# One sine half, one bank and two numerator groups moved at the start of a cosine-weighted attention and SwiGLU kernel

## The chip, the cores and the metric

The kernel runs on one core of one Trainium2 chip. A core has five engines that run at the same time, each with its own queue of instructions that it takes in order: TensorE (PE in the profile, with its weight loads as PEld), VectorE (DVE), ScalarE (ACT), GpSimd (POOL) and SyncE (SP). Instructions on different engines wait for each other through semaphores. Matrix products land in PSUM, which this kernel uses as seven banks: `psA` (two), `psG`, `psV` and `psC` (two each). DMAs are issued by SP or by POOL and run on 16 DMA engines. The metric is the time of one execution in microseconds on the device; lower is better.

## The reference

Two layers follow each other. The first is linear attention with cosine weights, for 8 batches, 8 heads, 576 positions, head size 64:

```python
phi(x) = concat(max(x, 0) * cos_w, max(x, 0) * sin_w)      # 64 -> 128 features
kv  = sum over s of phi(k)[s, f] * v[s, d];   z = sum over s of phi(k)[s, f]
out = (phi(q) @ kv) / (phi(q) @ z + 1e-6)
```

The second takes the 4608 rows of 512 (8 batches of 576), normalises each by its root mean square and a weight `g`, and applies a SwiGLU feed-forward with 1536 inner columns: `(silu(xn @ w_gate) * (xn @ w_val)) @ w_out`. Inputs and output are float32; the kernel multiplies in bfloat16.

## The kernel before, in words

**Blocks.** The feed-forward works on blocks of 512 rows. Block b (0 to 7) holds 512 rows of batch b as four tiles of 128; block 8 holds the batches' remaining 64 rows and runs between blocks 6 and 7. A block has 12 steps n = 0 to 11, each computing 128 of the 1536 inner columns, four matmuls for the gate into `psG[n % 2]` and four for the value into `psV[n % 2]` (L556); ACT takes the Silu of the gate (L575) and DVE multiplies it with the value into `hT` (L576). Then come four output steps, 12 to 15, of 12 matmuls each (L579) into `psC`, whose result ACT copies out (L286) and SP stores (L590, or L597 in block 0). The input of a block is `xnT`, the normalised rows transposed; there are two such buffers, used in turn, and every matmul of L556 reads all four tiles of its block.

**Attention alongside.** While block b is multiplied, the attention of batch b + 1 is made ready in between. A helper `at(blk, n, where, f, ...)` puts a piece of work into a slot of a step: "pe" ahead of the step's matmuls, "pre" behind them, "post" behind the step's own ACT and DVE work, or, in output steps, behind the store. Entries of one slot run in the order in which `at` was called. Each engine executes what it is given in this written order. The pieces for batch nb:

- `k_phi` (L292 on ACT for the sine half, L294 on DVE for the cosine half), `v_cast`, and `kvz_pe`, which makes kv and z in `psA`.
- `q_phi`: the two halves of phi of one q tile, then the transposition into `qpT`: by a DMA transpose (`q_tr_dma`, L346), or, for batch 1, by PE into a bank (`q_tr_pe`, L363) and a copy out of it (`q_tr_evac`).
- `nd_pe` (L449): numerators and denominators of one q tile, 8 matmuls into `psA`. `nd_post`: DVE's reciprocal and product (L489, L492, L499) into `xt`, which frees `psA` again.
- `x_sq` (ACT, L515) and a power on POOL (L520) for the root mean square; `x_norm` (DVE, L527); `x_tr_dma` (L540), a DMA transpose issued by SP into the next block's `xnT`.
- `load_kv` and `load_q`: the loads of a later batch, 1 MB or a little more each, issued by SP (by POOL for the first batches) into a ring of five buffers.

**Around the change.** Batch 1 is prepared late in block 0. Its last value step, `last_step`, makes kv, the numerators of q tile 0 and, in `q_tr(2, psV[0])`, the transposition of q tile 2. Block 0's output, `out_first`, is 48 matmuls numbered i = 0 to 47 over four banks; ahead of certain i stand pieces of batch 1: at 6, 11 and 19 the numerators of tiles 1, 2 and 3, at 9 the transposition of q tile 3, at 43 the last tile's transposition by PE into `psV[0]`.

Batch 2 is prepared in block 1. Its numerators stand ahead of steps 6, 8, 9 and 11, and the normalisation and `x_tr_dma` of each follow one step later (two for the first). In the "post" slot of step 12 stands also SP's load of batch 3's q (`load_q`, 1 MB), and in that of step 13 the load of a pair of q tails. For the later batches the steps are 4, 6, 8 and 10.

Of the kernel before, what the change touches and what calls it, by code (L numbers as in the profile page):

```python
# [17 lines left out]
def kernel(  # L18
# [28 lines left out]
    V, A, G = nc.vector, nc.scalar, nc.gpsimd  # L47
# [11 lines left out]
    psV = [ps.tile([P, 512], FP32, name=f"psV{i}") for i in range(2)]  # L59
# [15 lines left out]
    def wide(b):  # L75
        return b > 2
# [681 lines left out]
    def at(blk, n, where, f, *args):  # L758
        slots.setdefault((blk, n), {}).setdefault(where, []).append((f, args))
# [9 lines left out]
        at(0, 5 + c // 3, "post", k_phi, A, 1, c, 1)  # L769
    for j in range(4):  # L770
        at(0, (8, 8, 9, 10)[j], "post", q_phi, V, 1, j, 0)
        at(0, 8 + j, "post", q_phi, A, 1, j, 1)
        bank = (psC[0], psC[1], psV[0], psV[1])[j]
        if j < 2:
            at(0, 10 + j, "pe", q_tr_pe, 1, j, bank)
            at(0, 10 + j, "pre", q_tr_evac, V, 1, j, bank)
# [42 lines left out]
    for j, i in ((1, 6), (2, 11), (3, 19)):  # L819
        at(0, 12, i, x_first, j)  # L820
        at(0, 12, i, x_last, j - 1)
    at(0, 12, 9, q_tr, 3, psV[1])
    at(0, 12, 21, x_norm, 1, 3)
    at(0, 12, 21, load_q, 2)
    at(0, 12, 43, x_tr, 3, psV[0])
    for nb in range(2, B):
        b = nb - 1
        first = nb == 2
        for i, cs in enumerate(KCS5 if wide(nb) else KCS):
            kb, kn = ((0, 14), (0, 15), (1, 0), (1, 1))[i] if first else (b - 1, 12 + i)  # L830
            for c in cs:
                at(kb, kn, "post", k_phi, V, nb, c, 0)
                at(kb, kn, "post", k_phi, A, nb, c, 1)
        for i in range(2):
            vb, vn = ((0, 15), (1, 0))[i] if first else (b - 1, 13 + 2 * i)
            at(vb, vn, "post", v_cast, V, nb, (2 * i, 2 * i + 2))
        for j in range(4):
            late = j + (nb == 3)
            qb, qn = (b, 1 + j) if first else (b - (late < 2), (14 + late) % 16)
            at(qb, qn, "post", q_phi, V, nb, j, 0)  # L840
            at(qb, qn, "post", q_phi, A, nb, j, 1)
            at(qb, qn, "post", q_tr_dma, nb, j)
        kz = 3 if first else 2
        at(b, kz, "pe", kvz_pe, nb)
        at(b, kz, "pre", kvz_evac, A, nb)
        for j in range(4):
            n = ((6, 8, 9, 11) if first else (4, 6, 8, 10))[j]
            at(b, n, "pe", nd_pe, nb, j)
            at(b, n, "pre", nd_post, nb, j)
            at(b, n, "post", x_sq, nb, j)  # L850
            m = n + 2 if first and j == 0 else n + 1
            at(b, m, "post", x_norm, nb, j)
            at(b, m, "post", x_tr_dma, nb, j)
# [107 lines left out]
```

## Time and profile before

| what | value |
|---|---|
| median of 3 runs | 323.7 us (323.67 to 324.08) |
| the profiled execution | 323.82 us, span 322.0 us |
| mean granted TensorE clock | 0.999 |
| PE busy | 316.3 us, 98% of the span |
| DVE busy | 186.2 us, 58% |
| ACT busy | 166.0 us, 52% |
| POOL busy | 40.8 us, 13% |
| SP's DMA queue (q1) | 73110 packets, 41.25 MB, 62.6% of 16 engines' span |
| POOL's DMA queue (q0) | 6944 packets, 12.13 MB, 15.5% |

How to read the profile's lines. A row of the table of engines gives busy time, its share of the span, and the number of instructions. The chain that ended last is followed back from the last instruction to whatever released it, and is printed in order of time as start, length, engine, tile and line; while one engine is the bound, nearly all of it is on that engine. A timeline row has start, length, engine, line, operation, tiles (written tile first), the number of instructions merged, and in brackets the idle time of the engine before it and what ended it. "SPq" marks SP's issuing of a DMA: its length is that of the issue, and the transfer lands later. A row of DMA issues gives the transfer, its size and the time from issue to landing. A row of a window gives, for a stretch of time, its length, the busy time of PE, PEld, DVE, ACT and POOL with the number of instructions in brackets, the granted TensorE clock as a share of full speed, the share of the DMA engines and GB/s. All times count from the start of the span.

In time order: the stretch up to 33 us makes batch 0's attention and begins block 0; block 0's output runs from 42 to 55 us, block 1's value steps from 55 to 78 us, its output from 78 to 88 us, and block 2 begins at 88.3 us.

### The profile page before, as it was taken

What the parts mean: (1) busy time and instruction counts of PE and PEld (TensorE: products, weight loads), DVE (VectorE), ACT (ScalarE), POOL (GpSimd) and SP (SyncE); (2) the same over time, 40 slices, a digit from 0 to 9 for tenths busy, and PEclk for the clock granted to TensorE, in tenths of its full rate; (3) what the DMA queues carried; (4) which work ended last, traced back from release to release, by engine and by line L of the source; (5) the groups of instructions that cost most, each with busy time, mean ns of one, the idle gap of its engine ahead of it and who ended that gap; (6) DMA issues with size and microseconds to landing.
All of it is one profiled execution on the core that took longest, in us unless ns stands there. A gap on an engine that the chain in (4) does not pass through costs nothing.

```text
span 322.0 us, 6059 instructions
## 1 busy us (share of the span) xinstructions
PE 316.3 (98%) x2310; PEld 162.2 (50%) x2310; DVE 186.2 (58%) x382; ACT 166.0 (52%) x322; POOL 40.8 (13%) x79
## 2 busy tenths in 40 slices
PE   7899999999999999999999999999999999999996
PEld 2689564544455445444544445544544444444444
DVE  7976977768447772777457655781676034204420
ACT  5766665754575457455745575446544333223321
POOL 9771211002001100011001100100011000000000
PEclk9999999999999999999999999999999999999999
DMA  7999999778999989999799959994522500041002
GB/s 228 239 269 269 282 328 209 219 168 179 214 224 224 204 244 203 231 246 167 159 195 215 211 153 198 206 217 154 107 53 47 116 33 0 0 100 33 1 35 98
DMA packets 80091, 53.76 MB, mean 167 GB/s; under 512 B 52234, under 2 KB 74046, under 8 KB 80062
## 3 DMA queue, kind: packets, MB, share of 16 engines
q1 hardware_dynamic: 73110, 41.25, 62.6%
q0 software_dynamic: 6944, 12.13, 15.5%
q8 instruction: 18, 0.29, 0.4%
q14 instruction: 11, 0.09, 0.1%
q10 hardware_dynamic: 8, 0.00, 0.0%
HBM read 37.83 MB, written 9.44 MB: 147 GB/s over the span
## 4 chain that ended last, share of the span: by engine, by line
PE 94%; DMA 2%; ACT 1%; POOL 1%; DVE 1%; issue 0%; POOLq 0%; ACTq 0%
PE psC L579 27%; PE psG L556 27%; PE psV L556 27%; DMA vv<-in_v_dram 2%; PE psV L648 2%; PE psA L449 2%; PE psG L648 2%; PE psA L387 2%; PE psG L579 1%; PE psA L394 1%; PE psV L363 1%; PE psA L474 0%; ACT scr L515 0%; PE psG L430 0%; PE psC L546 0%; POOL raw L135 0%
## 5 line engine op out<-in xcount | busy, mean ns | idle before, releaser
L576 DVE TENSOR_TENSOR hT<-psV,sg 128x512 bf16<-128x512 f32 x99 | 68.2, 689 | 96.4 <-PE psV L556 64.9
L556 PE MATMUL psV<-xnT,wv 128*128 128x512 bf16 x352 | 90.3, 379 | 0.0
L556 PE MATMUL psG<-xnT,wg 128*128 128x512 bf16 x352 | 90.3, 379 | 0.0
L575 ACT ACTIVATE sg<-psG 128x512 f32<-128x512 f32 x99 | 58.6, 592 | 60.5 <-PE psG L556 57.7
L579 PE MATMUL psC<-wo,hT 128*128 128x512 bf16 (+1 forms) x408 | 88.8, 376 | 0.0
L579 PEld LDWEIGHTS <-hT 128*128 128x128 bf16 x456 | 43.1, 98 | 47.7
L556 PEld LDWEIGHTS <-wv 128*128 128x128 bf16 x400 | 39.0, 98 | 47.0
L556 PEld LDWEIGHTS <-wg 128*128 128x128 bf16 x400 | 36.9, 98 | 39.6 <-issue 0.2
L520 POOL TENSOR_TENSOR rs<-ms,mhalf 128x1 f32<-128x1 f32 x36 | 20.6, 572 | 194.1 <-ACT scr L515 193.9
L286 ACT COPY osb<-psC 128x512 f32<-128x512 f32 x32 | 18.8, 586 | 49.9 <-PE psC L579 49.9
L515 ACT ACTIVATE scr<-xt 128x513 bf16<-128x513 f32 x36 | 22.8, 634 | 22.6 <-DVE xt L499 21.7
L527 DVE SCALAR_TENSOR_TENSOR xn<-xt,rs,gb 128x512 bf16<-128x512 f32 (+1 forms) x37 | 26.9, 731 | 9.9 <-POOL rs L520 9.8
L292 ACT ACTIVATE kp<-raw,tab 128x256 bf16<-128x256 f32 (+2 forms) x51 | 28.8, 607 | 2.4 <-DMA raw<-in_k_dram 2.4
L499 DVE TENSOR_TENSOR xt<-psA,rec 128x512 f32<-128x512 f32 x36 | 24.9, 692 | 1.2
L292 ACT ACTIVATE qp<-raw,tab 128x512 bf16<-128x512 f32 (+1 forms) x36 | 23.4, 666 | 1.9 <-DMA raw<-in_q_dram 1.9
L294 DVE TENSOR_SCALAR kp<-raw,tab 128x256 bf16<-128x256 f32 (+2 forms) x53 | 20.2, 428 | 0.6 <-DMA raw<-in_k_dram 0.6
L294 DVE TENSOR_SCALAR qp<-raw,tab 128x512 bf16<-128x512 f32 (+1 forms) x34 | 15.5, 468 | 4.4 <-DMA raw<-in_q_dram 4.4
L449 PEld LDWEIGHTS <-qpT 128*128 128x128 bf16 x224 | 10.5, 97 | 7.0 <-DMA qpT<-qp 0.5
L288 DVE CAST vv<-raw 116x1280 bf16<-116x1280 f32 (+1 forms) x13 | 11.5, 881 | 1.8 <-DMA raw<-in_v_dram 1.8
L556 PE MATMUL psV<-xnT_tail,wv 128*128 128x512 bf16 x48 | 12.3, 379 | 0.0
L556 PE MATMUL psG<-xnT_tail,wg 128*128 128x512 bf16 x48 | 12.3, 379 | 0.0
L449 PE MATMUL psA<-kvzs,qpT 128*128 128x65 bf16 x224 | 11.4, 193 | 0.0
(102 smaller groups left out, 178.4 us busy)
## 6 DMA issues: line engine op xcount, KB each, us to landing
out_dram<-osb SPq DMA_DIRECT2D x27, 256.0 KB, 2.3
raw<-in_q_dram SPq DMA_DIRECT2D x6, 1024.0 KB, 9.2
raw<-in_k_dram SPq DMA_DIRECT2D x5, 1120.0 KB, 8.7
raw<-in_v_dram SPq DMA_DIRECT2D x5, 1120.0 KB, 9.7
raw<-in_k_dram POOLq DMA_DIRECT2D x2, 1152.0 KB, 19.4
raw<-in_v_dram POOLq DMA_DIRECT2D x2, 1152.0 KB, 15.9
out_dram<-osb SPq DMA_DIRECT2D x17, 128.0 KB, 2.6
wg<-in_moe_w_gate_dram POOLq DMA_DIRECT2D x3, 512.0 KB, 13.9
```

What stands on the lines that cost most here:

```text
L286: A.copy(out=o, in_=i)
L292: A.activation(out=out_ap, in_=in_ap, func=AF.Relu, scale=scale)
L294: eng.tensor_scalar(out=out_ap, in0=in_ap, scalar1=scale, scalar2=0.0, op0=ALU.mult, op1=ALU.max)
L449: nc.tensor.matmul(heads[:, g, hp, :], lhsT=qpT[:, h, j * P : (j + 1) * P], rhs=kvzs[b][:, g, hp * E : (hp + 1) * E], start=True, stop=True,)
L499: V.tensor_tensor(out=xt[:, 0:DM].rearrange("p (hp g d) -> p g hp d", g=2, d=D), in0=heads[:, :, :, 0:D], in1=rec[:, :, :].unsqueeze(3).to ...
L515: A.activation(out=scr[:, :], in_=xt[:, 0 : DM + 1], func=AF.Square, scale=1.0 / math.sqrt(DM), accum_out=ms[:, :],)
L520: G.tensor_tensor(out=rs[:, :], in0=ms[:, :], in1=mhalf[:, :], op=ALU.pow)
L527: V.scalar_tensor_tensor(out=xn_of[(b, j)][:, c], in0=x_of[(b, j)][:, c], scalar=rs_of[(b, j)][:, :], in1=gb[:, c], op0=ALU.mult, op1=ALU. ...
L556: nc.tensor.matmul(bank[:, cols[0] : cols[1]], lhsT=w[:, t, n * P : (n + 1) * P], rhs=x[:, t, cols[0] : cols[1]], start=(t == 0), stop=(t ...
L575: A.activation(out=sg[:, :], in_=g[:, 0:TB], func=AF.Silu)
L576: V.tensor_tensor(out=hT[:, n, :], in0=v[:, 0:TB], in1=sg[:, :], op=ALU.mult)
L579: nc.tensor.matmul(bank[:, 0 : cols[1] - cols[0]], lhsT=hT[:, n, j * P : (j + 1) * P], rhs=wo[:, n, cols[0] : cols[1]], start=(n == 0), st ...
```

## The change

Three constants and one bank differ.

- The sine half of phi of batch 1's q tile 3, on ACT, moves from the end of step 11 of block 0 (`last_step`) to the end of step 10, directly behind the same half of tile 2.
- The transposition of that tile by PE goes into `psV[0]`, which tile 2's used just before, and no longer into `psV[1]`.
- In block 1, the numerators of batch 2's tiles 2 and 3 go from steps 9 and 11 to steps 10 and 12. With them move `nd_post`, `x_sq`, and, one step behind, `x_norm` and `x_tr_dma`: for tile 2 to step 11, for tile 3 to step 13.

```diff
     for j in range(4):
         at(0, (8, 8, 9, 10)[j], "post", q_phi, V, 1, j, 0)
-        at(0, 8 + j, "post", q_phi, A, 1, j, 1)
+        at(0, (8, 9, 10, 10)[j], "post", q_phi, A, 1, j, 1)
...
-    at(0, 12, 9, q_tr, 3, psV[1])
+    at(0, 12, 9, q_tr, 3, psV[0])
...
         for j in range(4):
-            n = ((6, 8, 9, 11) if first else (4, 6, 8, 10))[j]
+            n = ((6, 8, 10, 12) if first else (4, 6, 8, 10))[j]
             at(b, n, "pe", nd_pe, nb, j)
             at(b, n, "pre", nd_post, nb, j)
             at(b, n, "post", x_sq, nb, j)
             m = n + 2 if first and j == 0 else n + 1
             at(b, m, "post", x_norm, nb, j)
             at(b, m, "post", x_tr_dma, nb, j)
```

## The prediction

> **What bounds the kernel now.** I read the page's table of engines first, then the chain that ended last around the two places that the diff touches (42 to 46 us; 71 to 97 us), then SP's instructions in order of time, because SP issues the transposes there, and last the landings of single transfers.
>
> From the page, then the chain in order of time (start, length, what):
>
> ```profile
> PE 316.3 (98%) x2310; PEld 162.2 (50%) x2310; DVE 186.2 (58%) x382; ACT 166.0 (52%) x322; POOL 40.8 (13%) x79
> ...
> 43.78 0.73 ACT scr L515 x2
> 44.50 0.62 ACT qp L292
> 45.12 0.04 issue
> 45.17 0.62 PE psV L363 x8
> ...
> 70.35 0.24 PE psA L449 x8
> ...
> 71.45 0.86 PE psV L556 x4
> 72.32 0.32 PE psA L449 x8
> ...
> 78.06 10.36 PE psC L579 x48
> 88.42 0.86 PE psG L556 x4
> ...
> 96.55 0.42 PE psA L449 x8
> ```
>
> PE is the bound, 98% busy: an edit pays only where the chain leaves PE, and hurts only where it makes PE wait. The chain leaves PE at 43 to 45 us: the transposition of q tile 3 (L363) follows ACT's sine half (L292). At 72.32 a numerator group takes 0.32 us where an undisturbed one takes 0.24 (70.35); at 96.55 0.42. Block 2 follows block 1's output matmuls at 88.42 with no gap.
>
> SP's instructions in order of time:
>
> ```profile
> 75.12 1.02 SPq L115 DMA_DIRECT2D raw<-in_v_dram  x2
> 76.23 2.63 SPq L540 DMA_TRANSPOSE xnT<-xn  x2
> 81.30 0.38 SPq L590 DMA_DIRECT2D out_dram<-osb  x1
> 81.77 1.22 SPq L540 DMA_TRANSPOSE xnT<-xn  x1
> 83.08 0.53 SPq L126 DMA_DIRECT2D raw<-in_q_dram  x1
> 83.89 0.36 SPq L590 DMA_DIRECT2D out_dram<-osb  x1
> 84.30 1.87 SPq L145 DMA_DIRECT2D rqt<-in_q_dram  x2
> ...
> 107.29 0.57 SPq L126 DMA_DIRECT2D raw<-in_q_dram  x1
> 109.40 5.31 SPq L540 DMA_TRANSPOSE xnT<-xn  x2
> ```
>
> Now the transpose of batch 2's fourth tile (81.77; I call it T) goes out **ahead** of batch 3's 1 MB q load (83.08). At 107 us another transpose goes out **behind** such a load, and how long each took, from issue to landing, is in the answers for their own stretches (q load at 107.29, transpose at 109.40, transpose at 73.80 with little queued ahead):
>
> ```profile
> raw<-in_q_dram SPq DMA_DIRECT2D x1, 1024.0 KB, 10.3
> ...
> xnT<-xn SPq DMA_TRANSPOSE x1, 8.6
> ...
> xnT<-xn SPq DMA_TRANSPOSE x1, 2.6
> ```
>
> 107.29+10.3 = 117.6 and 109.40+8.6 = 118.0: the transpose behind the load landed 0.4 us after it, not 2.6 us after its own issue. The stores agree: the one of 81.30 took 5.9 us (lands 87.2), that of 83.89, behind the q load, 7.4 (91.3), the tail load of 84.30 7.6 (91.9). The q load itself landed by 90.6, where DVE's wait for it ends (4.44 us before 90.61). So SP's transfers land very nearly in the order of issue.
>
> **The change part by part.** The sum is made against the profiled execution: 323.82 us with a span of 322.0, 0.1 above the median 323.7.
>
> *Sine half earlier, other bank.* One ACTIVATE of 0.71 us (L292) moves from 44.40 to behind the third's (38.26, ending 38.97). ACT idles 0.97 us there, until the Silu of 39.94 gets its bank, so 38.97 to 39.68 hides; if that idle time were missing, the Silu and PE's last output matmuls would be later by up to 0.71. At its old place ACT then just waits longer for xt (45.65). The transposition needs DVE's cosine half (ended 40.83) and the first value bank, whose previous content ACT copied out by 43.88 (42.87+1.01); PE reaches it at 44.86 (44.21 plus three matmuls of 0.216). So it starts at 44.86, not 45.17: 0.31 us at most. The next group is late no more than that: it needs xt of 44.85+0.69 = 45.54 and would come at 45.75. But block 1, at 54.59, loads weights 0.17 us late, and the third transpose of its input, issued at 50.28 with 4.2 us to landing, lands at 54.5. Its predecessors were delayed by POOL's batch-2 v load, issued at 39.18 and not moved. Gain between 0.05 and 0.31; I take 0.1, as the landing is the nearest limit.
>
> *Numerators spaced.* Tile 2's group goes one step on, tile 3's from the last value step to the first output step, with their xt, square, pow (POOL is idle over 1 us before each) and normalisation. PE's 0.08 us at 72.32 goes, since the xt that it waited for (71.49+0.69) is then long done. Tile 2's transpose moves from 77.6 to about 79.7 us and still queues behind the v load of 75.12 (8.6 us to landing, 83.7): costs nothing; without that load it would arrive 2 us later, with 8 to spare.
>
> *Tile 3 and SP's queue.* Before, step 12 of block 1 (its first output tile) issues store 0, T and the q load; T leaves for step 13, behind store 1. New order: store 0, q load, store 1, T, tail load. T's input: ACT's copy ends at 81.28, square and accumulator 0.82, pow 0.55, normalisation 0.75 give 83.4 to 83.7; store 1 holds SP until 84.25; T issues at 84.3 to 85.5. ACT's copy for store 1 had 0.78 us of idle time, so the inserted square costs it 0.04. Until T lands PE can't begin block 2 (every matmul there reads all four tiles), and behind PE's first weight load stands all the rest.
>
> Where does T land? The transfers up to and including T are the same set that ended with store 1 before, at 91.3. Lower bound: T can't land before the q load and store 1 have gone, and even the q load landed at 90.6 with T ahead of it; freed of T (the second of 85 to 86 us moved only 115 GB/s, the four after it 297 to 349) it gains some 1.2, then store 1 costs 256 KB at 340 GB/s = 0.8, and T its 1.2: 91.4 again, less what overlaps. Ends: 90.3 (all of T's length overlapped) and 91.9 (the next entry's landing). I take 91.0, less the 0.1 gained above, since the v load is issued relative to PE. PE starts 0.05 us after a landing (the transpose issued at 91.35 landed 5.2 us later, at 96.5, and released the group of 96.55): 90.95 against 88.26 for block 2's first matmul: **+2.7**. The 0.08 doesn't count then, as the landing sets the start. The q load lands about 1.1 us earlier, so batch 3's q tiles come earlier and PE's wait at 96.55 goes: 0.42-0.24 = **-0.2**. From there the chain shows PE alone.
>
> *Clock.* PE would idle from 87.9 to 90.95, some 3 us; the longest gap now in mid-kernel is about 1.1. At the end of the kernel the windows (PE busy in column 2, granted clock after POOL) show:
>
> ```profile
> 319.20:321.50 2.30, 0.04 (x1) 0.00 (x0) 0.26 (x1) 0.00 (x0) 0.00 (x0) 1.00 0.37 114
> 321.50:322.00 0.50, 0.00 (x0) 0.00 (x0) 0.00 (x0) 0.00 (x0) 0.00 (x0) 0.71 0.00 0
> ```
>
> 0.71 over half a us is full speed for 0.2 and half speed for 0.3: the clock halved 2.45 us after PE's last matmul. At the start, ten warm-up matmuls of 634 ns median (379 later) took 3.84 us, the last of them already at 379: full speed came after about 3.2 us of work. So a 3 us gap may halve the clock, and 3.2 us of work at half speed cost 1.6. Ends 0 and 1.7; I take **+1.6**, as 3 is beyond 2.45, though not by much, and one row says nothing of the phase.
> [...]
>
> Sum: 323.82 + 2.7 - 0.2 + 1.6 = 327.9, against the median of runs 327.8.
>
> **The rivals.**
> 1. *The same wait without the halved clock.* [...] 323.7+2.7-0.2 = 326.2, from 325.5 to 327.1 with T's bounds. [...]
> 2. *Not slower: T isn't held by the q load.* The place is the start of block 2. T issued at 84.3 with 2.6 us (transpose of 73.80) lands at 86.9; with 4.2 (50.28) at 88.5. Up to 88.2 PE loses nothing, and the time is 323.7-0.1-0.1-0.2 = 323.3, at best 323.1. Against it: 117.6 and 118.0, and 91.3 for a store issued right behind the same q load.
>    [...]
> 3. *A short wait.* T lands between 88.6 and 90, by overlap with the store and the load: 324 to 325.4, gap too short for the clock.
> 4. *A longer wait.* T takes the 8.6 us of the one at 109.40: 92.9, +4.6; 323.7+4.6-0.2+1.6 = 329.7.
>
> **How the numbers follow.** Chances: forecast 0.46, rival 1 0.34, rival 2 0.10, rival 3 0.05, rival 4 0.05. Predicted 327.8. Range 325.5 (rival 1, T at 90.3) to 328.9 (forecast, T at 91.9, clock 1.7); it leaves out rivals 2, 3 and 4. 0.2% is 0.65 us, about what can be told from no change. Rival 2 gives 323.1 to 323.6, mostly within that: faster 0.03, same 0.08, slower 0.89.
>
> **What would show it.** After: L292's fourth sine half near 39 us with nothing of ACT ahead of the transposition at 44.9; block 1's start within 0.3 us of before. SP: the q load at about 81.7, T at about 84.3, and T's landing near 91. PE idle some 3 us between the last output matmul of block 1 and L556 near 91, released by the transpose into xnT; a granted clock under 1.00 and 634 ns matmuls in the 3.4 us behind it. The group near 96 no longer released by qpT. Wrong if T lands before 88.2, if the idle stretch leaves the clock at 1.00 (then 326.2), or if later blocks show waits that they don't have now.

## The result and the profile after

The changed kernel takes 325.04 us (median of 8 runs, 324.64 to 325.46), the kernel before 323.89 us (8 runs, 323.0 to 324.58): a ratio of 1.0037, 95% interval 1.0024 to 1.005, so some 1.2 us slower. The profiled execution took 324.64 us with a span of 322.9. A second profile of each stands beside these below, from the experiments.

The table of engines and the chain in order of time, at the two places of the change:

```profile
PE 314.4 (97%) x2274; PEld 162.3 (50%) x2310; DVE 185.3 (57%) x382; ACT 166.0 (51%) x322; POOL 40.5 (13%) x79
...
43.97 0.65 PE psG L579 x3
44.62 0.45 PE psV L363 x8
45.06 0.43 PE psG L579 x2
...
69.62 0.24 PE psA L449 x8
...
82.81 0.72 DVE vv L288
83.53 5.54 DMA xnT<-xn
89.07 0.14 issue
89.21 1.02 PE psG L556 x4
...
97.51 0.25 PE psA L449 x8
```

The trace has 36 matmul records fewer than that of before (x2274 against x2310) for the same matmuls, so the two busy times of PE can't be compared. The sine half no longer stands in the chain: the transposition at 44.62 follows the three output matmuls ahead of it without a gap. But the chain now leaves PE from 73 to 89 us, and its longest stretch off PE there is a transfer: T, the transpose of batch 2's fourth tile, issued at 83.53 and landed at 89.07. (That the value cast of the `L288` row released T is the profile's inference; T's issue follows directly behind SP's issue of store 1, and in a run below T goes out at 83.90 before the same cast ends at 83.99.) Block 2's first matmul, at 88.26 before, is at 89.21, although everything ahead of it runs 0.7 us earlier than in the profile of before (0.4 of that from the first 35 us, where executions differ, 0.3 from the sine half).

SP's instructions, and what PE waited for (in total, times, longest):

```profile
80.49 0.38 SPq L590 DMA_DIRECT2D out_dram<-osb  x1
80.96 0.39 SPq L126 DMA_DIRECT2D raw<-in_q_dram  x1
83.08 0.36 SPq L590 DMA_DIRECT2D out_dram<-osb  x1
83.53 1.23 SPq L540 DMA_TRANSPOSE xnT<-xn  x1
```

```profile
PE psG L556 <- DMA xnT<-xn: 1.6, 1, 1.6
```

The order is the one that the diff makes: store 0, batch 3's q load, store 1, T. PE waits 1.6 us for T, once. The windows around that gap (PE's busy time in the second column, the granted clock after POOL's):

```profile
83.00:87.40 4.40, 4.40 (x22) 1.88 (x20) 2.18 (x5) 1.88 (x4) 0.00 (x0) 1.00 1.08 352
87.40:89.20 1.80, 0.22 (x1) 0.02 (x1) 0.47 (x1) 1.55 (x3) 0.00 (x0) 1.00 1.37 206
89.20:92.00 2.80, 2.74 (x12) 1.27 (x14) 0.80 (x2) 1.48 (x4) 0.00 (x0) 1.00 1.14 273
```

The clock stays at 1.00 through the gap and behind it.

### The profile page after: what moved, and what is told of

Read it like the earlier page. It is cut to its first block, busy times and chain, and to the rows that moved or that the text cites. A ratio compares the mean times of both kernels' runs of the same rounds, so it can differ in the third digit from the quotient of the medians.

```text
span 322.9 us, 6022 instructions
## 1 busy us (share of the span) xinstructions
PE 314.4 (97%) x2274; PEld 162.3 (50%) x2310; DVE 185.3 (57%) x382; ACT 166.0 (51%) x322; POOL 40.5 (13%) x79
## 4 chain that ended last, share of the span: by engine, by line
PE 89%; DMA 4%; DVE 3%; issue 2%; POOL 1%; ACT 1%; ACTq 0%; POOLq 0%; DVEq 0%
PE psV L556 26%; PE psG L556 26%; PE psC L579 24%; PE psV L648 2%; DMA vv<-in_v_dram 2%; PE psG L579 2%; PE psA L449 2%; PE psG L648 2%; PE psA L387 2%; DMA xnT<-xn 2%; DVE xn L527 1%; PE psA L394 1%; ACT scr L515 1%; PE psA L474 0%; PE psV L363 0%
## 5 line engine op out<-in xcount | busy, mean ns | idle before, releaser
L556 PE MATMUL psG<-xnT,wg 128*128 128x512 bf16 x337 | 88.5, 379 | 2.3 <-DMA xnT<-xn 1.6
L556 PE MATMUL psV<-xnT,wv 128*128 128x512 bf16 x344 | 89.6, 379 | 0.7 <-issue 0.2
L556 PEld LDWEIGHTS <-wv 128*128 128x128 bf16 x400 | 39.0, 98 | 47.0
L556 PEld LDWEIGHTS <-wg 128*128 128x128 bf16 x400 | 37.0, 98 | 41.7 <-issue 2.3
L556 PE MATMUL psV<-xnT_tail,wv 128*128 128x512 bf16 x48 | 12.3, 379 | 0.1
L556 PE MATMUL psG<-xnT_tail,wg 128*128 128x512 bf16 x46 | 12.0, 379 | 0.1
L288 DVE CAST vv<-raw 116x1280 bf16<-116x1280 f32 (+1 forms) x13 | 11.1, 857 | 0.0
```

Of the source, the lines that this page charges most:

```text
L556: nc.tensor.matmul(bank[:, cols[0] : cols[1]], lhsT=w[:, t, n * P : (n + 1) * P], rhs=x[:, t, cols[0] : cols[1]], start=(t == 0), stop=(t ...
```

## The experiments

Each run is compared with the kernel before on the same chip: 323.53 us (median of 23 runs) for the sine half with the bank, the spaced numerators alone, the steps 6, 8, 10, 11 and the q load behind T; 323.45 (13) for the q load ahead of T in the kernel before, the q load by POOL and the two further loads; 323.69 (23) for the sine half alone, the second profiles and the steps 5, 7, 9, 11.

### The parts alone

The sine half and the bank without the spaced numerators:

```diff
-            n = ((6, 8, 10, 12) if first else (4, 6, 8, 10))[j]
+            n = ((6, 8, 9, 11) if first else (4, 6, 8, 10))[j]
```

> The change without the spaced numerators: only ACT's sine half and the bank. Theory (the wait comes from the spacing alone): no wait of PE before block 2, the transposition starts at the end of the three matmuls ahead of it, 0.31 us earlier than before, and all of it is kept, as the profile of the changed kernel has block 1 begin 0.3 us earlier against its own start: 323.6 us against 323.9. Rival, the prediction's reading (block 1's start is held by the third transpose into its input): 0.1 us, 323.8. Rival (the sine half or the bank bears part of the loss): 324.2 or more.

Measured: 323.32 us, ratio 0.9989, interval 0.9977 to 1.0. The wait ahead of block 2 is not there, and block 2 begins near 87.5. The chain shows the same two rows as the changed kernel:

```profile
43.92 0.65 PE psG L579 x3
44.56 0.45 PE psV L363 x8
```

The sine half alone, with the transposition left in the second bank (`psV[1]`):

> The sine half moved, the transposition still in the second value bank, numerators as before. Theory (the bank bears no part): PE reaches the transposition with both halves and the bank ready, as with the first bank: 323.3 us, 0.3 under the kernel before. Rival (the first bank is what frees the transposition): the second bank is read by DVE until 44.2 us, so it waits, and the time stays at the kernel before's 323.5.

Measured: 323.26 us, ratio 0.9989, interval 0.9978 to 0.9999. The chain has the same rows once more:

```profile
43.58 0.65 PE psG L579 x3
44.22 0.45 PE psV L363 x8
```

So the bank bears no part. In the chains, the time from block 0's first `L556` row to block 1's is 21.94 us in the profile of before (32.97 to 54.91), 21.62 in the changed kernel (32.57 to 54.19) and 21.63 here (32.17 to 53.80): the sine half gives 0.3 us.

The spaced numerators alone (sine half and bank as before):

> Only the spaced numerators; sine half and bank as before. Theory: T lands behind batch 3's q load and store 1, PE waits for it ahead of block 2 for 1.3 to 1.7 us, and the parts add up: 0.3 us above the changed kernel, 325.3. Rival (the landing is a fixed time that the 0.3 us earlier PE only waits out): the same as the changed kernel, 325.0, with a wait of 1.3 us.

Measured: 325.02 us, ratio 1.0043, interval 1.0029 to 1.0057. T is issued at 84.00 and lands at 89.5, PE waits 1.5 us. So the loss is the spacing's. Against its own before this is 1.4 to 1.5 us, 0.2 to 0.3 more than the changed kernel's 1.2, as adding up would have it, but the intervals don't tell the two expectations apart.

### Tile 3's place or tile 2's?

Numerators ahead of steps 6, 8, 10 and 11, so that only tile 2 moves:

```diff
-            n = ((6, 8, 10, 12) if first else (4, 6, 8, 10))[j]
+            n = ((6, 8, 10, 11) if first else (4, 6, 8, 10))[j]
```

> Numerators of batch 2 ahead of steps 6, 8, 10 and 11, so tile 2 is spaced and tile 3 stands where it stood, T ahead of the q load. Theory (only T's place in SP's queue costs): no wait ahead of block 2; 0.3 us from the sine half and 0.08 from the numerators' wait at step 9: 323.5 us. Rival (tile 2's later transpose is what comes late): a wait ahead of block 2 as in the changed kernel, near 325.

Measured: 324.03 us, ratio 1.0015, interval 1.0005 to 1.0026. Neither expectation: there is no wait ahead of block 2, but a new one in front of tile 3's numerators. The timeline of DVE and PE there:

```profile
74.24 0.74 DVE L527 SCALAR_TENSOR_TENSOR xn<-xt,rs,gb 128x512 bf16<-128x512 f32 x1
74.90 0.16 DVE L489 TENSOR_SCALAR rec<-psA 128x8 f32<-128x8 f32 x1
75.09 0.20 DVE L492 RECIPROCAL rec<-rec 128x8 f32<-128x8 f32 x1
75.33 0.69 DVE L499 TENSOR_TENSOR xt<-psA,rec 128x512 f32<-128x512 f32 x1
...
76.07 0.40 PE L449 MATMUL psA<-kvzs,qpT 128*128 128x65 bf16 x8 [0.58 <-DVE xt L499]
```

Tile 1's normalisation now stands on DVE ahead of tile 2's division, which frees `psA` only at 76.02, one step after tile 2's numerators. Two groups one step apart cost 0.08 us of waiting in the kernel before, and 0.58 here.

### Is it the place behind the q load?

T where the change put it, but the q load issued directly behind T:

```diff
             at(b, m, "post", x_tr_dma, nb, j)
+            if first and j == 3:
+                at(b, m, "post", load_q, 3)
...
-                at(b, n, "post", load_q, nb)
+                if nb > 3:
+                    at(b, n, "post", load_q, nb)
```

> The changed kernel, but SP issues batch 3's q load directly behind T and not ahead of it; T's own issue stays where the change put it, near 83.5 us. Theory (SP's queue is served in order, T waits for the 1 MB ahead of it): T lands near 87, PE doesn't wait ahead of block 2, the q load lands 2.5 us later than in the changed kernel and PE's wait for batch 3's first q transpose near 96 us is back at 0.2 to 0.5: 323.7 us. Rival (T is late because it is issued one output step later, whatever stands ahead): it lands near 89 as in the changed kernel and the time stays 325.0.

Measured: 325.14 us, ratio 1.0043, interval 1.0029 to 1.0057. On T the theory holds: issued at 83.90, no earlier than in the changed kernel, it is in time, and block 2 begins at 87.81 with no wait. Store 1 is issued ahead of T here as in the changed kernel, so the store alone isn't what makes T late. On the time it fails. The q load, issued at 85.21, takes 7.0 us and lands at 92.2. What PE waits for now, and ACT's timeline behind it:

```profile
PE psG L556 <- ACT sg L575: 0.8, 1, 0.8
...
PE psA L449 <- DMA qpT<-qp: 0.5, 1, 0.5
```

```profile
92.19 0.72 ACT L292 ACTIVATE qp<-raw,tab 128x512 bf16<-128x512 f32 x1 [2.98 <-DMA raw<-in_q_dram]
92.82 0.58 ACT L575 ACTIVATE sg<-psG 128x512 f32<-128x512 f32 x1
```

ACT stands 2.98 us at batch 3's first sine half, and block 2's Silu, queued behind it, keeps its gate bank from PE for 0.8 us; the q transposes come 0.5 us late as well. So both transfers have a deadline near the start of block 2, and neither order on SP's queue served both with T issued at 83.5 to 83.9.

The reverse in the kernel before: nothing moved but the q load, one step earlier, ahead of T.

```diff
-        for which, n in zip("kvq", {1: (4, 8, 12), 2: (3, 5, 8)}.get(b, (0, 3, 6))):
+        for which, n in zip("kvq", {1: (4, 8, 11), 2: (3, 5, 8)}.get(b, (0, 3, 6))):
```

> The kernel before, with batch 3's q load one step earlier (step 11 of block 1), so ahead of T, which keeps its place and its issue at 81 to 82 us; nothing else is changed. Theory: T, though issued as early as before, lands behind the 1 MB, near 88.3 to 89.5 us against a start of block 2 near 88; PE waits 0.3 to 1 us: 323.9 to 324.5 us against 323.5. Rival (the later issue of T is what costs): no wait, 323.5.

Measured: 323.99 us, ratio 1.0016, interval 1.0005 to 1.0027. T, issued at 82.43, is over 1 us earlier than in the changed kernel and late all the same: PE has a gap of 0.69 us ahead of block 2, in the chain

```profile
87.91 0.69 issue
88.59 1.02 PE psG L556 x4
```

T's issue did come 1.0 us later against block 2 than in the kernel before, since SP took 1.55 us over the issue of store 0 ahead of it. But here T went out 5.5 us before block 1's output was done (87.91) and came late; with the place ahead of the q load it was in time when it went out 3.9 us before block 2's start (83.90 and 87.81). So the place decides.

### A queue of its own for the q load

The changed kernel with batch 3's q load issued by POOL:

```diff
-                at(b, n, "post", load_q, nb)
+                at(b, n, "post", load_q, nb, *((G,) if nb == 3 else ()))
```

> The changed kernel with batch 3's q load issued by POOL, at the same place in the order of work, so that it no longer stands in SP's queue; T is issued by SP near 83.5 us as in the changed kernel, with store 1 alone ahead of it. Theory (order within SP's queue): T shares the DMA engines with the q load but doesn't follow it, lands between 86 and 88 us, PE waits 0 to 0.5 us ahead of block 2: 323.4 to 324.3 us, if the q load itself isn't later than 90 us. Rival (the DMA engines' bytes decide, not the queue): T lands near 89 and the time stays 325.0.

Measured: 327.13 us, ratio 1.0133, interval 1.0079 to 1.0187. The theory in its narrow form falls, and the rival too, as the time isn't 325.0 but more. T is issued at 83.73 and PE starts at 91.28. The q load by POOL (issued at 81.87):

```profile
raw<-in_q_dram POOLq DMA_DIRECT2D x1, 1024.0 KB, 8.6
```

It lands at 90.4, T some 0.8 us behind, going by PE's start. Another queue didn't let T pass: the load that was issued first landed first, here too, and it took longer (8.6 us from issue to landing, against 6.4 in the changed kernel, from 80.96 to the end of DVE's wait for it at 87.39). Why T stayed behind a load on another queue is not shown: this run changed the queue alone. The windows of this run:

```profile
87.80:90.30 2.50, 0.00 (x0) 0.00 (x0) 0.00 (x0) 1.21 (x2) 0.00 (x0) 1.00 1.40 209
90.30:91.20 0.90, 0.00 (x0) 0.00 (x0) 0.49 (x1) 0.72 (x1) 0.00 (x0) 0.52 1.31 211
91.20:97.10 5.90, 5.60 (x13) 2.05 (x15) 1.08 (x2) 1.71 (x4) 0.00 (x0) 0.50 1.00 148
97.10:99.00 1.90, 1.90 (x44) 1.52 (x43) 1.08 (x2) 0.70 (x2) 0.00 (x0) 0.99 0.72 138
```

PE's gap is 3.5 us, and the clock halves 2.5 us into it and stays so for 6.8 us. Of these, 0.9 us fall in the gap; the other 5.9 us are work at half speed and cost 2.9 us, an estimate from the clock of 0.50. This execution took 330.07 us with a mean granted clock of 0.99, the three others 326.6, 326.7 and 327.5 with 1.0, 1.0 and 0.995.

### How long a gap halves the clock?

The changed kernel with a further load directly behind the q load, into a buffer that nothing reads: 0.5 MB, and 0.75 MB.

```diff
+    extra = one.tile([P, 4, 4 * D], FP32, name="extra")
+    def load_extra():
+        nc.sync.dma_start(out=extra[:, :, :], in_=q_rows(3)[:, 0:4, :])
...
                 at(b, n, "post", load_q, nb)
+                if nb == 3:
+                    at(b, n, "post", load_extra)
```

> The changed kernel with a further load of 0.5 MB (half of batch 3's q rows, into a buffer that nothing reads) directly behind the q load and so ahead of T. Theory: T lands 1.5 us later at 330 GB/s, PE's wait ahead of block 2 grows from 1.6 to 3.1 us and the time by as much, 326.5, with the clock at full speed. Rival, the prediction's reading of the kernel's end (the clock halves 2.45 us after PE's last matmul): the granted clock is 0.5 in the 3 us behind the wait, 634 ns matmuls, 1.6 us more, 328.1.

> As the 0.5 MB load, with 0.75 MB. Theory: T lands 2.3 us later than in the changed kernel, PE waits 3.9 us, 327.3 with the clock at full speed throughout. Rival (2.45 us of idle PE halve the clock): 328.9 and a granted clock of 0.5 behind the wait. If this one shows the halved clock and the 0.5 MB one doesn't, the limit lies between 3.1 and 3.9 us, or depends on where the wait falls in some period.

Measured: 329.35 us for 0.5 MB (ratio 1.0166, interval 1.0116 to 1.0217; single runs 326.64, 329.1, 329.61, 329.95) and 329.11 us for 0.75 MB (1.0186, 1.0146 to 1.0225; 328.77 to 330.69). The profiled executions (326.64 and 329.34 us), 0.5 MB first:

```profile
87.60:90.80 3.20, 0.02 (x1) 0.00 (x0) 0.49 (x1) 1.81 (x3) 0.00 (x0) 1.00 1.22 286
90.80:94.20 3.40, 3.25 (x15) 1.57 (x17) 1.08 (x2) 1.73 (x4) 0.00 (x0) 1.00 1.15 252
```

```profile
87.80:91.80 4.00, 0.19 (x1) 0.00 (x0) 0.49 (x1) 1.82 (x3) 0.00 (x0) 1.00 1.19 298
91.80:95.20 3.40, 3.04 (x7) 1.17 (x9) 0.00 (x0) 1.21 (x2) 0.00 (x0) 0.50 1.17 258
95.20:97.00 1.80, 1.80 (x10) 0.79 (x9) 1.08 (x2) 0.67 (x2) 0.00 (x0) 0.99 0.00 0
```

A gap of 3.3 us left the clock at full speed in the profiled execution. A gap of 3.9 us halved it, at its very end, for 3.4 us of work. The three other runs with 0.5 MB are 2.5 to 3.3 us longer than the profiled one. Their mean granted clocks are known, though their gaps aren't: 0.995, 0.99 and 0.99, against 0.999 for the profiled run. A mean of 0.994 goes with the 3.4 us at half speed of the profiled 0.75 MB run, 0.99 with the 6.8 us of the POOL run. So, going by the means, the clock halved in three of the four runs with 0.5 MB, and in all four with 0.75 MB (0.99 to 0.994): one and the same kernel does both. Both loads moved T as the queue's order has it: PE's gap grew from 1.6 us by 1.7 and 2.3.

### Second profiles, and a variant

> The kernel before, for a second profile. The prediction took T's place from one execution, in which store 0 landed at 87.2 us, the q load at 90.6 and store 1 at 91.3, 0.8, 2.3 and 3.0 us from the start of block 2 at 88.3. Theory (that execution had a slow stretch of the DMA queue): here the q load lands within 1.6 us of block 2's start, as in the run with the sine half alone (89.1 against 87.5). Rival (it is the rule for this kernel): again 2.3 us behind it.

> The changed kernel, for a second profile and beside the others on one chip. T lands 1.4 to 1.8 us behind the end of block 1's output matmuls, the clock stays at 1.00, 325.0 us. If T's landing swings by over 1 us from execution to execution, the wait here differs by as much from the 1.6 us of the first profile.

Measured: the kernel before 323.18 us in its one execution, span 321.4. Store 1, issued at 83.07, this time takes

```profile
out_dram<-osb SPq DMA_DIRECT2D x1, 256.0 KB, 6.9
```

so it lands at 90.0, 2.5 us behind block 2's start at 87.44, where it was 3.0 in the profile that the prediction used. Store 0 took 4.7 us, not 5.9. So that profile had the queue about half a us behind; the q load, 1.8 us behind block 2's start, lies between the two expectations. The changed kernel again: 324.88 us, ratio 1.0039, interval 1.0025 to 1.0052, T lands at 88.8, PE waits 1.6 us and the clock stays at 1.00.

Numerators two steps apart without moving T:

```diff
-            n = ((6, 8, 10, 12) if first else (4, 6, 8, 10))[j]
+            n = ((5, 7, 9, 11) if first else (4, 6, 8, 10))[j]
```

> Sine half and bank as in the change, and batch 2's numerators two steps apart the other way round, ahead of steps 5, 7, 9 and 11, so T keeps its place ahead of the q load. Theory (spacing itself is free if T isn't moved): no wait of PE in front of a numerator group (0.08 us at step 9 with the sine half alone, 0.6 at step 11 with 10 and 11) and none ahead of block 2: 323.2 us, at most 0.1 under the sine half and bank alone. Rival (two steps apart costs in itself, or the first group comes ahead of its q transpose): 323.6 or more, with a wait in front of the group of step 5.

Measured: 323.15 us, ratio 0.9985, interval 0.9975 to 0.9996: all four groups are free of waits and T is in time. It is the fastest version measured, 0.5 us under the kernel before. From the sine half alone (323.26 on the same chip) its difference is within the spread. The chain's rows of the groups:

```profile
64.49 0.24 PE psA L449 x8
68.18 0.24 PE psA L449 x8
71.88 0.24 PE psA L449 x8
75.58 0.24 PE psA L449 x8
```

## Why the prediction was right or wrong

*Direction and mechanism: right.* T goes behind batch 3's q load in SP's queue, lands after block 1's output is done, and PE waits for it once, ahead of block 2. Taking T's place, the q load's place and the parts apart each gave the time that this mechanism asks for, except where the late q load, or two numerator groups one step apart, brought a wait of their own.

*The sine half: under-sized.* Its 0.31 us of gap was seen; the prediction kept 0.1, holding block 1's start to be bound by the third transpose into its input, issued at 50.28 with 4.2 us to landing. In the changed kernel that transpose, issued at 49.56 and again with 4.2 us to landing, lands at 53.8, 0.2 us ahead of block 1's first matmul (54.03), and the runs with the sine half alone keep 0.2 to 0.4 us. The bank at no cost: right. The sine half hidden in ACT's idle time: right (ACT's Silu at 39.54 still waits for PE, 0.36 us).

*T's landing: the step that failed.* "I take 91.0", so +2.7 us and a gap of about 3. Measured 89.07, a gap of 1.6 us. The term that was mis-sized is what the q load gains once T no longer stands ahead of it: "it gains some 1.2". DVE's wait for that load shows where it landed, in the profile that the prediction used, in the second one of before and in the changed kernel:

```profile
90.61 0.49 DVE L294 TENSOR_SCALAR qp<-raw,tab 128x512 bf16<-128x512 f32 x1 [4.44 <-DMA raw<-in_q_dram]
...
89.27 0.49 DVE L294 TENSOR_SCALAR qp<-raw,tab 128x512 bf16<-128x512 f32 x1 [4.34 <-DMA raw<-in_q_dram]
...
87.39 0.49 DVE L294 TENSOR_SCALAR qp<-raw,tab 128x512 bf16<-128x512 f32 x1 [2.22 <-DMA raw<-in_q_dram]
```

Before, the load landed 2.3 and 1.8 us behind block 2's start (88.26 and 87.44); in the changed kernel it landed 0.2 us before block 1's output was done (87.62, where PE's gap begins). So it gained 2.6 us against the first profile of before and 2.1 against the second, not 1.2. Of the 1.4 us that the prediction missed, 0.5 came with the one execution that it used, whose queue was that much later against PE than in the second, and 0.9 is the gain itself. The step behind it was right: store 1 and T took 1.7 us from the q load's landing to T's (87.39 to 89.07), where the prediction had 0.8 and 1.2 less 0.4 of overlap. How much of the gain is T's own transfer, how much a slower load behind it, and how much the load's issue, 1.5 us earlier against PE (80.96 and 83.08), no run separates.

*The clock: +1.6 that didn't come.* The term hung on a gap of 3 us. The gap of 1.6 us left the clock alone in both profiles, and in all 12 runs of the changed kernel the mean granted clock was 0.999 or 1.0. The reading behind the term, 2.45 us from PE's last matmul to the halved clock at the kernel's end, is no fixed limit either: a 3.3 us gap in mid-kernel left full speed, one of 3.5 halved it after 2.5 us, and one of 3.9 after 3.8. But as three of four runs with the 0.5 MB load halved it, "may halve" was fair for a gap of that size. The term's upper end, 1.7, and the 3.4 us of 634 ns matmuls that were to show the halved clock come from no row of before. What the runs showed in their place: a clock of 0.50 for 3.4 us of work behind the gap of 3.9 us (matmuls of 631 ns, median), which makes some 1.7 us as an estimate, and of 0.50 to 0.52 for 6.8 us from inside the gap of 3.5 us on, 5.9 of them work. No run shows a phase or a period on which the halving hangs, as the prediction and the expectation for the 0.75 MB load have it; shown is that one kernel, with the 0.5 MB load, kept a mean clock of 0.999 in one run and had 0.99 to 0.995 in three.

*PE's wait near 96 us: right in the profile used* (0.42 became 0.25), but the second profile of before doesn't have it (0.24 there), so it is no steady gain.

*The sum.* With the terms as measured: +1.6 (wait), -0.3 (sine half) and -0.1 (numerators at step 9) give +1.2, against medians 1.15 apart. The forecast of 327.8 and its range, 325.5 to 328.9, lie above it. What came is the third rival, "a short wait", T between 88.6 and 90, which had been given 0.05: the prediction's lower bound of T was too high, because what T costs the load behind it was under-sized, and because one profile's landing times were taken as the kernel's.

## What to carry to other kernels

Moving a step moves its DMA past others on the queue: write out the queue's order before and after, and look for the large load that the small transfer now stands behind (here 128 KB behind 1 MB, and a wait of 1.6 us). A landing time read from one profile may be off by half a us and more against the compute around it (here 2.3 and 1.8 us behind block 2's start, for one load in two profiles of one kernel); take it from two profiles, and ask what the large load gains when the small transfer no longer stands ahead of it (here 2.1 to 2.6 us, with its issue 1.5 us earlier), before adding a second cost, such as a clock step, that only sets in if the first is large. When two transfers on one queue each have a deadline at the same place, swapping them may only move the wait: here from 1.6 us for T to 0.8 and 0.5 us behind the q load, 325.04 us and 325.14.

## What the runs showed of the hardware that wasn't expected

- A load on POOL's queue that was issued 1.4 us ahead of a store and 1.9 us ahead of a transpose on SP's queue landed ahead of the transpose as it did on SP's own: 90.4 against some 91.2 us.
- The granted clock in mid-kernel: full speed through a gap of 3.3 us in one execution, half speed from 2.5 us into a gap of 3.5 us in another, and from 3.8 us into a gap of 3.9 us in a third. Half speed lasted 3.4 and 6.8 us. Four runs of one kernel, with the 0.5 MB load, had mean clocks of 0.999, 0.995, 0.99 and 0.99 and took 326.64 to 329.95 us.
- The same four transfers on one queue (store 0, T, the q load, store 1) were through 8.6 us after the issue of store 0 with the transpose last, and 9.5 and 10.0 us after it, in the two profiles of before, with the transpose third from last.
- A 1 MB load landed 2.1 to 2.6 us sooner, against PE, when a 128 KB transpose no longer stood ahead of it on its queue; its issue came 1.5 us earlier.
